# Residual adds moved to GpSimd, an order on its queue, wide PSUM buffers and a new prologue in a fused convolution and phase-mixing kernel

## Chip, cores, metric

One core of a Trainium2 chip. The metric is device time in microseconds (us), the median of several executions. Ratios are the mean time of one kernel's runs over that of the other's runs of the same rounds, so they are not quite the ratio of the medians quoted beside them. The kernel before ran beside each of the three groups of experiments, each group on another chip, and its median there lies between 1477.4 and 1481.4 us. Each kernel was profiled once, so a stretch of a profile stands for one execution.

## The reference, cut to what matters

```python
# x: (8, 4224, 192); weight: (8 heads, 7 taps)
w = softmax(weight)                                  # per head
x = causal 7-tap convolution of x with w, per head   # "attn_out"
theta = x @ w_theta
zr, zi = x * cos(theta), x * sin(theta)
y = w_tok_r @ zr + w_tok_i @ zi                      # over the 4224 tokens
u = x + y
out = u + relu(u @ w_ch)
```

Nearly all arithmetic is the token mix `y`: two 4224 x 4224 matrices against 1536 columns (8 batches x 192).

## The kernel before: the parts that matter

Tokens are cut into 33 chunks of 128. Each chunk is convolved (`conv`), transposed, multiplied by `w_theta`, sent through sine and cosine, and multiplied with x into seven operands `z`. The token mix runs in 58 steps. A step takes up to 11 chunks and two blocks of 128 output rows, by a seven-product scheme whose weight blocks are transposed and combined on VectorE. Partial sums go to `part` in memory and come back 17 steps later. Steps 41 to 57 are final: they add x (the residual add), then cast, transpose and multiply by `w_ch`. TensorE's results land in buffers of the PSUM memory, and VectorE or ScalarE has to copy each out, or "evacuate" it, before this program uses the buffer again. A buffer of one bank holds 512 float32 per partition here.

```python
mmpool = tile_pool(name="mmps", bufs=4, space=PSUM)       # four one-bank buffers
def transposed(u):                                        # 6 transposes, one copy on ScalarE
    tp = bank("tp", F16) ...
# class Step
def load_w(self, name):                                   # four of these a step
    for a in range(NQ):
        nc.gpsimd.dma_start(out=st[...], in_=w[...])      # float32 -> float16, no order given
def add_x(self, i):
    to = part[...][tb] if self.late else self.pv[i]       # late: the last five steps
    nc.gpsimd.dma_start(out=to[:, cols], in_=xs[rows, cols], accum_op=ALU.add)
def give(self, y, i, h, copies):                          # empties an accumulator: pv += y (VectorE)
def cast(self, i, g):
    self.ub[i, g] = wk.tile([P, GC], F16, name="ub", tag="ub", bufs=4)   # ScalarE
def output(self, i, g, k):                                # half of a group: 4 matmuls, 1 VectorE op
# prologue: bands of the convolution by 15 VectorE operations; while the first chunks
# are made, everything that TensorE can't yet do is replaced by idle matmuls on `spare`
```

`in_order("pe" | "dve" | "act", ins)` chains the instructions of those engines in program order. Instructions without it, all of GpSimd's, are placed by the scheduler of the framework.

Of the kernel before, what the change touches and what calls it, by code (L numbers as in the profile page):

```python
# [10 lines left out]
ALU = mybir.AluOpType  # L11
# [5 lines left out]
def kernel(  # L17
# [69 lines left out]
    def act(ins):  # L87
        return in_order("act", ins)

    constp = ctx.enter_context(tc.tile_pool(name="const", bufs=1))  # L90
# [7 lines left out]
        tc.tile_pool(name="mmps", bufs=4, space=bass.MemoryType.PSUM)  # L98
# [7 lines left out]
    def bank(name, dtype=F32):  # L106
        return mmpool.tile([P, PC if dtype == F32 else 2 * PC], dtype,
                           name=name, tag="mm")
# [6 lines left out]
    ident = constp.tile([P, P], F16, name="ident")  # L115

    def channel_weights(w, name):
        R = D - P
        t = constp.tile([P, 4, D], F16, name=name)
        nc.vector.memset(t[:, 1:3, :], 0.0)  # L120
        nc.gpsimd.dma_start(out=t[:, 0, :], in_=w[0:P, :])
        nc.gpsimd.dma_start(out=t[0:R, 1, :], in_=w[P:D, :])
        nc.gpsimd.dma_start(out=t[R:P, 2, :], in_=w[0:R, :])
        nc.gpsimd.dma_start(out=t[:, 3, :], in_=w[R:D, :])
        return t
# [5 lines left out]
    def channel_mix(tT, k, w):  # L131
        v = bank("v")
        for b in range(2):
            for i in range(2):
                pe(nc.tensor.matmul(  # L135
                    v[:, b * D : (b + 1) * D], lhsT=tT[:, 3 * k + b + i, :],
                    rhs=w[:, 2 * b + i, :], start=(i == 0), stop=(i == 1),
                ))
        return v[:, 0 : 2 * D]

    def transposed(u):
        tp = bank("tp", F16)
        for k in range(6):
            pe(nc.tensor.transpose(  # L144
                tp[:, k * P : (k + 1) * P], u[:, k * P : (k + 1) * P], ident
            ))
        uT = wk.tile([P, 6, P], F16, name="uT", tag="uT")
        act(nc.scalar.activation(  # L148
            out=uT[:, :, :].rearrange("p k s -> p (k s)"), in_=tp[:, 0 : 6 * P],
            func=AT.Copy,  # L150
        ))
        return uT
# [3 lines left out]
    class Chunk:  # L156
# [25 lines left out]
        def conv(self, hp):  # L182
            if hp == 0:
                self.z = zpool.tile([P, 7, HN], F16, name="z", tag="z")
                self.x = self.z[:, T2 : T2 + 2, :].rearrange("p t n -> p (t n)")
            pc = bank("pc")
            for hh in range(2):
                h = 2 * hp + hh
                for half in range(2):
                    pe(nc.tensor.matmul(  # L190
                        pc[half * 2 * Q : (half + 1) * 2 * Q,
                           hh * B * G : (hh + 1) * B * G],
                        lhsT=bands[:, h, :, :].rearrange("p a m -> p (a m)"),
                        rhs=self.xw[:, half, :, h * G : (h + 1) * G],
                        start=True, stop=True,
                    ))
            act(nc.scalar.activation(  # L197
                out=self.x.rearrange("p (b d) -> p b d", d=D)[
                    :, :, hp * 2 * G : (hp + 1) * 2 * G
                ].rearrange("p b (h g) -> p h b g", h=2),  # L200
                in_=pc[:, 0 : 2 * B * G].rearrange("p (h b g) -> p h b g", h=2, b=B),
                func=AT.Copy,
            ))
            if hp == H // 2 - 1:
# [6 lines left out]
        def transpose(self, g):  # L211
            self.xT[g] = transposed(self.x[:, g * GC : (g + 1) * GC])

        def theta(self, g, k):
            v = channel_mix(self.xT[g], k, wth).rearrange(
                "p (b h e) -> p b h e", b=2, h=2
            )
            b0 = g * GB + 2 * k
            for first, bias in ((Z11, half_pi[:]), (Z21, None)):
                o = self.z[:, first : first + 2, :].rearrange(  # L220
                    "p h (b e) -> p b h e", e=HD
                )[:, b0 : b0 + 2, :, :]
# [18 lines left out]
        def tasks(self):  # L241

            for hp in (0, 2):
                yield lambda hp=hp: [self.conv(hp), self.conv(hp + 1)]
            for g in range(NG):
                yield lambda g=g: self.transpose(g)
            for g in range(NG):
                for k in range(2):
                    yield lambda g=g, k=k: self.theta(g, k)
# [17 lines left out]
    class Step:  # L267


        def __init__(self, t):  # L270
# [8 lines left out]
            self.blocks = ("11", "21", "22", "12") if self.pair else ("11", "12")  # L279
            self.st, self.w, self.ub, self.uT, self.pv = {}, {}, {}, {}, []  # L280

        def load_w(self, name):
            tb = self.tbs[int(name[0]) - 1]
            w = (moe_w_tok_r, moe_w_tok_i)[int(name[1]) - 1]
            st = wpool.tile([P, NQ, NW * Q], F16, name="st", tag="st", bufs=4)
            n = self.n * Q
            for a in range(NQ):
                t0 = token(self.ks[0], a)
                nc.gpsimd.dma_start(  # L289
                    out=st[a * Q : (a + 1) * Q, :, 0:n],  # L290
                    in_=w[tb * P : (tb + 1) * P, t0 : t0 + n]
                    .rearrange("(bt i) s -> i bt s", bt=NQ),
                )
            self.st[name] = st
# [4 lines left out]
        def turn(self, name):  # L299
# [3 lines left out]
                self.st[name][:, :, 0 : self.n * Q]  # L303
# [35 lines left out]
        def add_x(self, i):  # L339

            if self.late:
                to = part[(self.t // NU - 1) % 2][self.tbs[i], :, :]
            else:
                to = self.pv[i]
            rows = slice(self.tbs[i] * P, (self.tbs[i] + 1) * P)
            for cols in (slice(0, HN), slice(HN, N)) if self.late else (slice(0, N),):
                nc.gpsimd.dma_start(  # L347
                    out=to[:, cols], in_=xs[rows, cols], accum_op=ALU.add
                )
# [61 lines left out]
        def cast(self, i, g):  # L411
            self.ub[i, g] = wk.tile([P, GC], F16, name="ub", tag="ub", bufs=4)
# [7 lines left out]
        def output(self, i, g, k):  # L420
            pk = self.pv[i][:, g * GC + k * 2 * D : g * GC + (k + 1) * 2 * D]
            dve(nc.vector.scalar_tensor_tensor(  # L422
                out=pk, in0=channel_mix(self.uT[i, g], k, wch), scalar=0.0, in1=pk,
                op0=ALU.max, op1=ALU.add,
            ))
            if k == 1:
                rows = slice(self.tbs[i] * P, (self.tbs[i] + 1) * P)
                nc.sync.dma_start(
                    out=out[g * GB : (g + 1) * GB, rows, :].rearrange("b s d -> s b d"),
                    in_=self.pv[i][:, g * GC : (g + 1) * GC].rearrange(  # L430
                        "p (b d) -> p b d", d=D
                    ),
                )

        def outputs(self):
# [3 lines left out]
            for i in range(len(self.tbs)):  # L439
                at = ((-self.time / 7 + 0.6, 1.2) if late else (0.7, 12.7))[i]  # L440
                cast, turn, mix = (1, 2.6, 4.4) if late else (2, 3.6, 5.4)
                for g in range(NG):
# [3 lines left out]
                    for k in range(2):  # L446
                        found.append((d + mix + 0.7 * k,
                                      lambda i=i, g=g, k=k: self.output(i, g, k)))
# [8 lines left out]
    def step_events(t):  # L457
# [11 lines left out]
        if t + 2 < NSTEP:  # L469
            nxt = steps[t + 2]  # L470
            for j, name in enumerate(nxt.blocks):
                found.append(((0.3, 1.3, 2.3, 4.3)[j], lambda name=name: nxt.load_w(name)))
# [4 lines left out]
        if t >= NU - 2:  # L477
# [4 lines left out]
            for k in (k for k in range(NK) if start[k] == t + 1 and k >= NW):  # L482
                pos = [0, .5, 1.3, 1.5, 2.1, 2.3, 2.5, 2.7, 3.1, 3.15, 3.4, 3.6]
# [14 lines left out]
    spare = bank("spare")  # L498
    noise = zpool.tile([P, PC], F16, name="noise", tag="z")
    nc.vector.memset(noise, 0.0)  # L500
    masks = wk.tile([2 * WR, KS, 2, Q], F16, name="masks", tag="ub", bufs=4)
    nc.gpsimd.memset(masks, 1.0)
    for k in range(KS):
        nc.gpsimd.affine_select(
            out=masks[:, k, :, :], in_=masks[:, k, :, :], pattern=[[WR, 2], [1, Q]],
            channel_multiplier=-1, base=HALO - KS + 1 + k,
            compare_op=ALU.is_equal, fill=0.0,
# [3 lines left out]
    for a, lo in ((0, True), (1, False)):  # L511
# [4 lines left out]
        )  # L516
    wmax = constp.tile([P, H], F32, name="wmax")
    nc.vector.tensor_reduce(out=wmax, in_=wsb, axis=mybir.AxisListType.X, op=ALU.max)
    nc.vector.tensor_tensor(
        out=wsb, in0=wsb, in1=wmax[:, :].unsqueeze(2).to_broadcast([P, H, KS]),  # L520
        op=ALU.subtract,
    )
    nc.scalar.activation(out=wsb, in_=wsb, func=AT.Exp)
    nc.scalar.activation(out=wmax[:, 0:1], in_=wsb[:, 0, 0:1], func=AT.Sin)
    wsum = constp.tile([P, H], F32, name="wsum")
    nc.vector.tensor_reduce(out=wsum, in_=wsb, axis=mybir.AxisListType.X, op=ALU.add)
    nc.vector.tensor_scalar_add(out=wsum, in0=wsum, scalar1=1e-9)
    wrcp = constp.tile([P, H], F32, name="wrcp")
    nc.vector.reciprocal(out=wrcp, in_=wsum)
    wbf = constp.tile([P, H, KS], F16, name="wbf")  # L530
    nc.vector.tensor_tensor(
        out=wbf, in0=wsb, in1=wrcp[:, :].unsqueeze(2).to_broadcast([P, H, KS]),
        op=ALU.mult,
    )
    taps = wk.tile([2 * WR, KS, Q], F16, name="taps", tag="uT")
    nc.vector.tensor_tensor(
        out=taps, in0=masks[:, :, 0, :], in1=masks[:, :, 1, :], op=ALU.add
    )
    btmp = wk.tile([2 * WR, 2, H, Q], F16, name="btmp", tag="ub", bufs=4)
    for k in range(KS):  # L540
        nc.vector.tensor_tensor(
            out=btmp[:, 1 if k else 0],
            in0=taps[:, k, :].unsqueeze(1).to_broadcast([2 * WR, H, Q]),
# [124 lines left out]
```

## Time and profile before

| | before |
|---|---|
| time, median | 1480.2 us |
| TensorE busy | 97% of the span |
| idle TensorE | 44 us, plus 16 us of spare matmuls |
| from the last token-mix matmul to the end | 14.0 us |

Read it from TensorE, which is full from 120 us on but for one dip and the tail. Only the idle time of TensorE can be won. The prediction shows the lines.

### The profile page before, as it was taken

What the parts mean: (1) busy time and instruction counts of PE and PEld (TensorE: products, weight loads), DVE (VectorE), ACT (ScalarE), POOL (GpSimd) and SP (SyncE); (2) the same over time, 40 slices, a digit from 0 to 9 for tenths busy, and PEclk for the clock granted to TensorE, in tenths of its full rate; (3) what the DMA queues carried; (4) which work ended last, traced back from release to release, by engine and by line L of the source; (5) the groups of instructions that cost most, each with busy time, mean ns of one, the idle gap of its engine ahead of it and who ended that gap; (6) DMA issues with size and microseconds to landing.
All of it is one profiled execution on the core that took longest, in us unless ns stands there. A gap on an engine that the chain in (4) does not pass through costs nothing.

```text
span 1479.8 us, 25342 instructions
## 1 busy us (share of the span) xinstructions
PE 1435.6 (97%) x10083; PEld 902.6 (61%) x10083; DVE 980.7 (66%) x1120; ACT 385.9 (26%) x664; POOL 604.5 (41%) x1096
## 2 busy tenths in 40 slices
PE   6899999999999999999999999998799999999997
PEld 3565666666666666666666666665466666666665
DVE  5885645454558787775666668778476667666676
ACT  5881111111135353000000015254021212222134
POOL 9743424242444542433324254553444333333330
PEclk9999999999999999999999999999999999999999
DMA  9997757464699999887868699999999989998675
GB/s 130 216 206 148 135 99 153 93 148 94 147 226 220 237 216 256 186 195 173 200 163 208 152 199 213 216 286 293 189 233 253 226 206 224 202 218 189 142 170 158
DMA packets 241318, 281.96 MB, mean 191 GB/s; under 512 B 76336, under 2 KB 209456, under 8 KB 241200
## 3 DMA queue, kind: packets, MB, share of 16 engines
q0 software_dynamic: 173280, 111.20, 54.0%
q1 hardware_dynamic: 67920, 169.14, 32.2%
q8 instruction: 79, 1.29, 0.3%
q14 instruction: 39, 0.32, 0.1%
HBM read 245.49 MB, written 108.13 MB: 239 GB/s over the span
## 4 chain that ended last, share of the span: by engine, by line
PE 84%; DMA 9%; POOL 4%; DVE 2%; issue 1%; ACT 0%; SPq 0%; DVEq 0%; POOLq 0%; ACTq 0%
PE y L394 77%; PE v L135 4%; DMA xw<-in_x_dram 3%; DMA st<-in_moe_w_tok_r_dram 3%; PE tp L144 2%; POOL st L289 2%; DMA st<-in_moe_w_tok_i_dram 2%; PE pc L190 1%; DMA part<-xs 1%; POOL xw L177 1%; DVE pv L359 1%; DMA xw<-xw 0%; DMA part<-pv 0%; DVE z L237 0%; DVE z L231 0%
## 5 line engine op out<-in xcount | busy, mean ns | idle before, releaser
L394 PE MATMUL y<-z,wt 128*128 128x384 f16 x7656 | 1312.1, 327 | 24.7 <-DVE pv L359 19.7
L394 PEld LDWEIGHTS <-wt 128*128 128x128 f16 x7656 | 738.1, 98 | 482.7 <-issue 31.5
L359 DVE TENSOR_TENSOR pv<-y,pv 128x768 f32<-128x768 f32 x324 | 308.9, 953 | 429.5 <-PE y L394 414.5
L289 POOL DMA_DIRECT2D st<-in_moe_w_tok_r_dram x448 | 244.2, 566 | 355.0 <-DVE wt L301 302.9
L289 POOL DMA_DIRECT2D st<-in_moe_w_tok_i_dram x448 | 243.7, 562 | 349.6 <-DVE wt L301 296.4
L301 DVE STREAM_TRANSPOSE wt<-st 128x1408 f16<-128x1408 f16 (+7 forms) x224 | 326.6, 1463 | 10.9 <-DMA st<-in_moe_w_tok_r_dram 8.5
L148 ACT ACTIVATE uT<-tp 128x768 f16<-128x768 f16 x132 | 105.5, 817 | 321.8 <-PE tp L144 321.8
L313 DVE TENSOR_TENSOR wt<-wt 128x1408 f16<-128x1408 f16 (+7 forms) x216 | 173.6, 804 | 10.1 <-PE y L394 6.6
L197 ACT ACTIVATE z<-pc 128x384 f16<-128x384 f32 x132 | 58.4, 504 | 384.2 <-PE pc L190 384.0
L357 ACT ACTIVATE pv<-y 128x768 f32<-128x768 f32 x66 | 53.8, 816 | 275.2 <-PE y L394 274.7
L135 PEld LDWEIGHTS <-uT 128*128 128x128 f16 x1056 | 93.4, 98 | 34.9 <-ACT uT L148 3.8
L177 POOL DMA_DIRECT2D xw<-in_x_dram x132 | 76.7, 594 | 50.5 <-DMA st<-in_moe_w_tok_r_dram 18.1
L422 DVE SCALAR_TENSOR_TENSOR pv<-v,pv 128x384 f32<-128x384 f32 x132 | 71.4, 548 | 24.5 <-PE v L135 24.0
L226 ACT ACTIVATE z<-v,half_pi 128x384 f16<-128x384 f32 x132 | 77.7, 589 | 32.3 <-PE v L135 31.2
L237 DVE TENSOR_TENSOR z<-z 128x768 f16<-128x768 f16 x132 | 73.6, 557 | 7.3 <-DMA xs<-z 2.4
L413 ACT ACTIVATE ub<-pv 128x768 f16<-128x768 f32 x66 | 52.2, 835 | 71.8 <-DVE pv L359 71.7
L135 PE MATMUL v<-wch,uT 128*128 128x192 f16 x528 | 63.8, 246 | 2.6 <-ACT uT L148 2.6
L231 DVE TENSOR_TENSOR z<-z 128x1536 f16<-128x1536 f16 x66 | 60.0, 950 | 9.1 <-ACT z L226 9.0
L226 ACT ACTIVATE z<-v 128x384 f16<-128x384 f32 x132 | 65.5, 497 | 0.0
L135 PE MATMUL v<-wth,uT 128*128 128x192 f16 x528 | 62.5, 248 | 0.8 <-ACT z L226 0.8
L347 POOL DMA_DIRECT2D pv<-xs x24 | 22.1, 935 | 71.6 <-ACT ub L413 29.3
L190 PE MATMUL pc<-xw,bands 96*64 96x192 f16 x528 | 35.4, 254 | 4.4 <-DMA xs<-z 1.9
(45 smaller groups left out, 195.3 us busy)
## 6 DMA issues: line engine op xcount, KB each, us to landing
part<-pv SPq DMA_DIRECT2D x79, 768.0 KB, 4.1
pv<-part SPq DMA_DIRECT2D x79, 768.0 KB, 6.5
out_dram<-pv SPq DMA_DIRECT2D x66, 384.0 KB, 4.5
st<-in_moe_w_tok_r_dram POOLq DMA_DIRECT2D x280, 88.0 KB, 5.1
st<-in_moe_w_tok_i_dram POOLq DMA_DIRECT2D x280, 88.0 KB, 3.9
pv<-xs POOLq DMA_DIRECT2D x24, 768.0 KB, 6.8
xs<-z SPq DMA_DIRECT2D x132, 96.0 KB, 4.6
xw<-in_x_dram POOLq DMA_DIRECT2D x121, 96.0 KB, 4.8
```

Of the source, the lines that this page charges most:

```text
L135: pe(nc.tensor.matmul(v[:, b * D : (b + 1) * D], lhsT=tT[:, 3 * k + b + i, :], rhs=w[:, 2 * b + i, :], start=(i == 0), stop=(i == 1),))
L148: act(nc.scalar.activation(out=uT[:, :, :].rearrange("p k s -> p (k s)"), in_=tp[:, 0 : 6 * P], func=AT.Copy,))
L177: nc.gpsimd.dma_start(out=self.xw[lo : lo + n, h, :, :], in_=x[:, t0 : t0 + n, :].rearrange("b s d -> s b d"),)
L226: act(nc.scalar.activation(**args))
L231: dve(nc.vector.tensor_tensor(out=o, in0=xv, in1=o, op=ALU.mult))
L237: dve(nc.vector.tensor_tensor(out=z[:, o, :], in0=z[:, a, :], in1=z[:, b, :], op=ALU.subtract))
L289: nc.gpsimd.dma_start(out=st[a * Q : (a + 1) * Q, :, 0:n], in_=w[tb * P : (tb + 1) * P, t0 : t0 + n] .rearrange("(bt i) s -> i bt s", bt=NQ),)
L301: dve(nc.vector.transpose(self.w[name][:, 0 : self.n, :, :], self.st[name][:, :, 0 : self.n * Q] .rearrange("p bt (c j) -> p c bt j", j=Q),))
L313: dve(nc.vector.tensor_tensor(out=self.w[name][:, 0 : self.n, :, :], in0=self.w[a][:, 0 : self.n, :, :], in1=self.w[b][:, 0 : self.n, :, : ...
L359: dve(nc.vector.tensor_tensor(out=o, in0=yv, in1=o, op=ALU.add))
L394: pe(nc.tensor.matmul(y[cn][:, q, 0:BH], lhsT=self.w[wn][:, c, :, :].rearrange("p bt i -> p (bt i)"), rhs=chunks[k].z[:, zn, q * BH : (q + ...
L422: dve(nc.vector.scalar_tensor_tensor(out=pk, in0=channel_mix(self.uT[i, g], k, wch), scalar=0.0, in1=pk, op0=ALU.max, op1=ALU.add,))
```

## The change

The intent: keep residual adds out of the DMA engines, let the loads of x pass weight loads, shorten the prologue, and halve the number of evacuations by wider PSUM buffers. The same token-mix matmuls run in the same order. Cut to its core:

```diff
+    def pool(ins):
+        return in_order("pool", ins)
-        tc.tile_pool(name="mmps", bufs=4, space=bass.MemoryType.PSUM)
+        tc.tile_pool(name="mmps", bufs=2, space=bass.MemoryType.PSUM)
-        return mmpool.tile([P, PC if dtype == F32 else 2 * PC], dtype,
+        return mmpool.tile([P, 2, PC if dtype == F32 else 2 * PC], dtype,
   # conv, theta, output: 8 matmuls into one two-bank tile, evacuated by one instruction
+    def evacuate(out, in_, by_dve=False): ...
+            self.xT[g] = transposed(..., 0 < self.k < 3 or (self.k, g) == (0, 1))   # VectorE
-        def load_w(self, name):      # 4 a step, 4 DMAs each, 4 buffers
+        def load_w(self, m):         # 2 a step, 4 DMAs each, 2 buffers twice as large
+                pool(nc.gpsimd.dma_start(...))
+            if not self.late:
+                xr = wk.tile([P, N], F16, name="xr", tag="xr", bufs=1)
+                nc.sync.dma_start(out=xr, in_=xs[rows, :])
+                pool(nc.gpsimd.tensor_tensor(out=self.pv[i], in0=self.pv[i], in1=xr, op=ALU.add))
+                return
+            ... pool(nc.gpsimd.dma_start(out=part[...], in_=xs[...], accum_op=ALU.add))
-            self.ub[i, g] = wk.tile([P, GC], F16, name="ub", tag="ub", bufs=4)
+            self.ub[i, g] = wk.tile([P, GC], F16, name="ub", tag="ub", bufs=2)
   # prologue: bands by 32 small matmuls instead of 15 VectorE operations; w_theta by plain
   # DMA and a VectorE cast
-            if i < 3:
-                idle(left)
+            if i < 2:
+                idle(min(left, 1))
```

## The prediction

> **What bounds the kernel now.** I read the page's busy shares and slices first.
>
> ```profile
> span 1479.8 us, 25342 instructions
> PE 1435.6 (97%) x10083; PEld 902.6 (61%) x10083; DVE 980.7 (66%) x1120; ACT 385.9 (26%) x664; POOL 604.5 (41%) x1096
> PE   6899999999999999999999999998799999999997
> ```
>
> TensorE is the bound. Its idle time is 1479.8 - 1435.6 = 44.2 us, in three places: the first slices, two slices past the middle, the last one. Any gain must come from there, or from matmuls that are no work: the kernel runs 51 matmuls on a tile `spare` to keep TensorE busy while it has no data (16.0 us in the windows). Then windows, cut where chunk 0's first convolution starts (12.2), where chunk 3's starts (35.27), and where TensorE has become full (120); a quiet stretch; and the dip:
>
> ```profile
> core 0: us, PE busy (x) PEld busy (x) DVE busy (x) ACT busy (x) POOL busy (x), PEclk, DMA share, GB/s
> 12.20:35.27 23.07, 20.01 (x162) 11.38 (x162) 9.48 (x17) 16.58 (x35) 21.80 (x41) 0.93 1.06 148
> 35.27:120.00 84.73, 73.67 (x648) 48.51 (x648) 75.05 (x105) 67.92 (x137) 53.24 (x98) 1.00 1.10 212
> 740.00:777.00 37.00, 37.00 (x230) 22.26 (x229) 22.67 (x21) 0.00 (x0) 10.74 (x20) 1.00 0.67 164
> 1023.00:1056.00 33.00, 19.83 (x105) 10.96 (x103) 16.76 (x19) 2.46 (x6) 11.67 (x20) 0.90 1.07 269
> 1056.00:1450.00 394.00, 394.00 (x2868) 259.40 (x2867) 274.91 (x332) 89.27 (x114) 146.70 (x252) 1.00 0.89 204
> ```
>
> The quiet stretch gives 37.00/230 = 160.9 ns for a 128x384 matmul with its weight load hidden, and no idle time: nothing to gain there. The stretch from 1056 to 1450 has none either. So the ledger of lost time is:
> - lead, 0 to 12.2: nothing useful, 12.2 us lost;
> - chunks 0 to 2, 12.2 to 35.27: 20.01 busy, of which the same windows for the spare matmuls show 11.43, so 8.6 useful of 23.07: 14.5 lost;
> - chunks 3 to 10, 35.27 to 120: 84.73 - 73.67 = 11.1 lost;
> - dip, 1023 to 1056: 33.00 - 19.83 = 13.2 lost;
> - tail, 1443 to 1480: 37.00 minus 28.86 busy = 8.1 lost; about 1 us elsewhere.
>
> That is some 60 us, so about 1420 us of useful TensorE work. This floor is not touched by the change: same matmuls, same columns.
>
> The waits of TensorE in the whole run say who ends the idle time, and the timeline of the dip shows the worst one (1045.43):
>
> ```profile
> PE y L394 <- DVE pv L359: 19.7, 11, 6.0
> PE spare L580 <- POOL ident masks.py:199: 6.8, 1, 6.8
> PE y L394 <- DVE z L231: 3.3, 4, 1.5
> ```
> ```profile
> 1044.42 0.96 DVE L359 TENSOR_TENSOR pv<-y,pv 128x768 f32<-128x768 f32 x1 [8.92 <-DMA st<-in_moe_w_tok_i_dram]
> 1045.30 1.63 DVE L301 STREAM_TRANSPOSE wt<-st 128x1408 f16<-128x1408 f16 x1
> 1045.43 5.01 PE L394 MATMUL y<-z,wt 128*128 128x384 f16 x22 [6.04 <-DVE pv L359]
> ```
>
> TensorE waits for VectorE to empty an accumulator, and VectorE sat 8.92 us because weight loads were late. Why late? The source view of the residual adds:
>
> ```profile
> L347 POOL DMA_DIRECT2D pv<-xs x24: 898/912/1260, 1037.4 to 1339.8; - x24
> L347 POOL DMA_DIRECT2D part<-xs x18: 797/1132/2428, 952.8 to 1118.4; - x18
>   POOL st L289: 21.7, 14
> ```
>
> The 18 accumulating DMAs into `part` belong to the last five steps and stand in the program at steps 49 to 53 of 58: a step of this stage takes 29 us (the chain repeats from 1072.8 to 1101.8 to 1130.8) and step 53 starts near 1400, so they stand at some 1290 us or later. They ran from 952.8: nothing ordered GpSimd's queue, so they were hoisted into the stretch that also loads x for the last chunks. Weight-load issues waited 21.7 us behind L347; from 960 to 1050 the DMA view has 286 GB/s and 8 to 9 us to landing for weights, against 122 GB/s and 3.5 to 5.1 between 150 and 400.
>
> **What the Trainium skill says.**
> - "GPSIMD Engine Reference", section "Elementwise — side-by-side cycle accounting": a two-input add costs about 2.6 cycles per element, 4497 ns for 2048 float32. An estimate for 1536 columns: 4497 x 1536/2048 = 3.4 us. The trace of before has no GpSimd add to compare.
> - "SBUF — State Buffer", section "SBUF: two separate sides": GpSimd and VectorE share a port pair under an exclusive lock, which a VectorE op with two SBUF inputs also takes. So an add can hold up a weight sum (L313, 0.8 us) or a product for up to 3.4 us. Before shows no instance.
> - "DMA: Bandwidth & Descriptors", section "Anatomy of one DMA": many descriptors can be emitted before the incremental cost shows. The trace agrees: weight-load issues cost 543 ns at the median, x loads with some two to three times as many rows 582.
> - "TensorE: Matmul & The Clock Gate", section "The HAM clock gate": the clock is halved unless TensorE has been busy for a window of about 3.4 us. The trace agrees in kind: the granted clock is 0.93 from 12.2 to 35.27 and 0.90 in the dip.
>
> **The change, part by part.**
> 1. *Order on GpSimd, and adds there.* Weight loads, late accumulates and the new adds are chained in program order, so the 18 accumulates leave the dip. The 24 direct ones (768 KB) become plain 384 KB loads plus an add. Weight loads merge, 896 issues to about 450, near 0.58 us each: GpSimd saves some 230 us of issue and spends 24 x 3.4 = 82 us on adds. GpSimd doesn't bound steady state (11 of 37 us), so only the dip counts. I keep 3.5 us of its 13.2 for adds that block VectorE and for accumulates now in steps 49 to 53. Gain 9.7.
> 2. *Bands on TensorE.* Before, 15 VectorE operations from 6.61 build the bands, ready at about 12.2. After: the softmax part still ends near 5.5, three small VectorE operations at 0.2 make the taps by 6.4, 32 tiny matmuls at about 0.07 (the 96x64 band loads took 0.31 for eight) take 2.3, the two-engine copy 0.5: 9.5 or so. Gain 2.5.
> 3. *Chunks 0 to 2.* ScalarE is the latency: per chunk 4 copies (0.87 a pair), 8 sines (0.85 a pair, from 28.70 to 29.55), 2 transposed copies (1.51): 6.7 us chained, plus spare matmuls in TensorE's order. After, half of chunk 0's copies and both transposed copies of chunks 1 and 2 go to VectorE, which is free here (9.48 of 23.07), and most spares go. I work the three out as 3.5, 6 and 6.5 us = 16 instead of 23.1, so 7.4 lost instead of 14.5. Chunk 2's load, which TensorE waited 1.5 us for, is issued some 5 us sooner. Gain 7.
> 4. *Chunks 3 to 10.* Two-bank evacuation: a chained 768-column copy is 0.755 against 0.87 for two of 384; per chunk 2 x 0.115 + 4 x 0.1 = 0.6 us less ScalarE. But VectorE is busy 75.05 of 84.73 and loses no work there, and DMA is already at 1.10. Gain 2 of the 11.1.
> 5. *Two wide PSUM buffers instead of four.* Neutral in steady state; in the tail, where transposes and outputs alternate, it costs about 1.
>
> Sum: 9.7 + 2.5 + 7 + 2 - 1 = 20.2; I round up to 23 because the freed GpSimd queue should also bring weights earlier, where VectorE's 90% hides small waits. 1480.2 - 23 = 1457.
>
> **Rivals.**
> - *The adds cost more than the dip gives back.* 24 locks of 3.4 us beside a VectorE that is 70% busy (274.91 of 394). Against it: an accumulator may be emptied up to one run later, 22 x 0.161 = 3.5 us, so most locks are hidden. If each cost 0.5 us, 12 us return: about 1469.
> - *A cold clock.* With few spare matmuls, chunks 0 to 2 may run at half clock: 8.6 useful us become up to 17, partly under ScalarE's latency. Costs up to 6: about 1463.
> - *DMA bounds the start.* For: the chain that ended last runs through x and weight transfers until about 97 us. Against: before 40 us, landing times are only 2.6 to 4.3. Then the gains of 2 to 4 vanish later: about 1468.
> - *All goes well.* Start loss 18 where parts 2 to 4 leave 26, dip and adds nearly nothing: about 1446.
>
> **Range and chances.** Over 2% faster needs less than 1450.6, thus 29.6 us out of a ledger of 60 of which tail and lead keep about 18: it needs the fourth rival. I give it 0.25. A slowdown of 2% would need some 50 us of new waits: 0.02. Range 1445 to 1469.
>
> **What would show it.** Right: no TensorE dip between 950 and 1080; accumulates into `part` only after about 1250; chunk 0's first convolution near 9.7 and chunk 3's near 26; GpSimd adds near 3.4 us; TensorE still full from 120 to the tail. Wrong: TensorE idle behind VectorE in the steps with adds, adds far above 3.4 us, a granted clock well under 0.93 early on, chunk 3's convolution waiting for x, or loss between 35 and 120 grown beyond 11.

## The result, and the profile after

The changed kernel takes 1479.85 us (1479.5 to 1480.68, 4 runs) against 1480.25 us: ratio 0.9999, 95% interval 0.9982 to 1.0016. Nothing was gained. First the page of the kernel after (span, TensorE's busy tenths, its granted clock in tenths):

```profile
span 1478.3 us, 24435 instructions
PE   6899999999999999999999999998999999999996
PEclk7999999999999999999999999999999999999998
```

The dip past the middle is milder, the last slice is emptier, and the first slice has a clock of 0.7. The windows of the kernel after, cut at its own first convolution, at chunk 3's, at 120, and around the dip:

```profile
core 0: us, PE busy (x) PEld busy (x) DVE busy (x) ACT busy (x) POOL busy (x), PEclk, DMA share, GB/s
9.22:34.33 25.11, 17.47 (x137) 10.37 (x138) 13.14 (x24) 11.58 (x15) 16.86 (x30) 0.71 1.26 176
34.33:120.00 85.67, 77.55 (x656) 50.31 (x656) 76.58 (x105) 64.21 (x86) 33.83 (x60) 0.97 0.99 205
1000.00:1056.00 56.00, 48.67 (x346) 30.32 (x345) 48.20 (x45) 15.65 (x20) 24.00 (x26) 0.97 0.91 228
1056.00:1440.00 384.00, 384.00 (x2806) 253.39 (x2805) 311.38 (x268) 87.63 (x113) 143.94 (x151) 1.00 0.84 195
```

Both programs run the same 7656 token-mix matmuls in the same order. So the start of the k-th in one trace can be set against the start of the k-th in the other, which is a better ruler than windows. The view of that line alone gives the first and last start, of the kernel before and of the kernel after:

```profile
L394 PE MATMUL y<-z,wt x7656: 322/326/527, 23.7 to 1465.8; 128*128 128x384 f16 x197
```
```profile
L404 PE MATMUL y<-z,wt x7656: 322/326/528, 23.2 to 1458.1; 128*128 128x384 f16 x197
```

At the last of these matmuls the changed kernel is 7.7 us ahead. At the end it is 1.5 us ahead. The whole account, from the two traces (matmuls counted from 0; each row is the time between two marks):

| stretch | before | after | change | predicted |
|---|---|---|---|---|
| lead, to the first convolution | 12.22 | 9.22 | -3.0 | -2.5 |
| chunks 0 to 2, to chunk 3's first convolution | 23.05 | 25.11 | +2.1 | -7 |
| to token-mix matmul 252 | 79.46 | 79.14 | -0.3 | -2 |
| to matmul 5400 | 905.05 | 906.01 | +1.0 | 0 |
| the dip, to matmul 5600 | 50.92 | 43.11 | -7.8 | -9.7 |
| to the last, matmul 7655 | 395.09 | 395.47 | +0.4 | 0 |
| tail, to the end | 14.04 | 20.25 | +6.2 | +1 |
| sum | 1479.8 | 1478.3 | -1.5 | -20.2 |

So the dip and the lead paid nearly as forecast. The first chunks and the tail took it back. The waits of TensorE in the whole run of the kernel after (total, times, longest) show two kinds that before had little or nothing of:

```profile
PE y L404 <- DVE pv L369: 11.8, 7, 5.2
PE tp L153 <- ACT z L233: 6.3, 10, 1.3
PE v L138 <- ACT uT L148: 4.4, 4, 1.6
PE y L404 <- DVE z L238: 3.1, 3, 1.5
PE v L138 <- ACT z L233: 3.1, 3, 1.2
```

`tp` waits for sines and cosines (L233) although a transpose reads none of their results. What it needs is the PSUM buffer that they still read: with two buffers, a group of matmuls takes the one that the group two places ahead had. In the tail (from 1455 us), ScalarE's waits before and after are:

```profile
ACT uT L148 <- PE tp L144: 9.0, 6, 3.1
ACT ub L413 <- DVE pv L359: 1.4, 2, 1.1
```
```profile
ACT ub L423 <- PE tp L153: 7.7, 4, 3.2
ACT uT L148 <- PE tp L153: 1.9, 1, 1.9
```

Before, no cast (`ub`) waited for a transpose. After, casts do: with two cast buffers, a cast must wait until the transposes of the cast before the last have read theirs. In the dip, VectorE and GpSimd of the kernel after in order of time (lines of other operations left out):

```profile
1028.26 4.98 DVE L238 TENSOR_TENSOR z<-z 128x1536 f16<-128x1536 f16 x2
1029.31 3.10 POOL L351 TENSOR_TENSOR pv<-pv,xr 128x1536 f32<-128x1536 f32 x1
...
1035.54 0.95 DVE L369 TENSOR_TENSOR pv<-y,pv 128x768 f32<-128x768 f32 x1
...
1036.54 1.95 PE L404 MATMUL y<-z,wt 128*128 128x384 f16 x6 [5.20 <-DVE pv L369]
```

Two products that take 1.82 us in e4, where no GpSimd add runs, took 4.98 beside a GpSimd add of 3.10. VectorE was not idle before it emptied the accumulator; it came to it late, and TensorE waited 5.20 us, of which the slowed products made some 3.2.

### The profile page after: what moved, and what is told of

Same layout as the page of the kernel before. It is cut to its first block, busy times and chain, and to the rows that moved or that the text cites. A ratio compares the mean times of both kernels' runs of the same rounds, so it can differ in the third digit from the quotient of the medians.

```text
span 1478.3 us, 24435 instructions
## 1 busy us (share of the span) xinstructions
PE 1435.8 (97%) x10086; PEld 904.9 (61%) x10086; DVE 1030.6 (70%) x1050; ACT 361.8 (24%) x461; POOL 435.3 (29%) x655
## 3 DMA queue, kind: packets, MB, share of 16 engines
HBM read 245.49 MB, written 108.13 MB: 239 GB/s over the span
## 4 chain that ended last, share of the span: by engine, by line
PE 91%; DVE 3%; ACT 2%; DMA 1%; POOL 1%; issue 1%; SPq 0%; DVEq 0%; ACTq 0%; POOLq 0%
PE y L404 82%; PE v L138 5%; PE tp L153 3%; PE pc L196 2%; DVE z L238 1%; ACT z L233 1%; DVE z L244 1%; POOL st L294 1%; DVE pv L369 1%; POOL xw L183 1%; DMA xw<-in_x_dram 1%; DMA part<-pv 0%; DVE wt L319 0%; DMA xw<-xw 0%; DVE wt L307 0%
## 5 line engine op out<-in xcount | busy, mean ns | idle before, releaser
L307 DVE STREAM_TRANSPOSE wt<-st 128x1408 f16<-128x1408 f16 (+7 forms) x224 | 326.4, 1462 | 3.9 <-DMA st<-in_moe_w_tok_r_dram 2.1
L294 POOL DMA_DIRECT2D st<-in_moe_w_tok_r_dram x232 | 132.4, 579 | 490.8 <-DVE wt L307 473.4
L294 POOL DMA_DIRECT2D st<-in_moe_w_tok_i_dram x232 | 132.4, 579 | 473.9 <-DVE wt L307 460.4
L319 DVE TENSOR_TENSOR wt<-wt 128x1408 f16<-128x1408 f16 (+7 forms) x216 | 227.2, 1052 | 10.1 <-PE y L404 6.6
L148 ACT ACTIVATE z<-pc 128x768 f16<-128x768 f32 x65 | 52.8, 812 | 386.5 <-PE pc L196 386.5
L367 ACT ACTIVATE pv<-y 128x768 f32<-128x768 f32 x66 | 53.6, 812 | 278.1 <-PE y L404 271.7
L433 DVE SCALAR_TENSOR_TENSOR pv<-v,pv 128x768 f32<-128x768 f32 x66 | 62.3, 948 | 26.9 <-PE v L138 24.1
L351 POOL TENSOR_TENSOR pv<-pv,xr 128x1536 f32<-128x1536 f32 x24 | 75.5, 3147 | 0.5 <-DMA xr<-xs 0.3
L233 ACT ACTIVATE z<-v,half_pi 128x768 f16<-128x768 f32 x66 | 59.5, 901 | 40.7 <-PE v L138 40.7
L233 ACT ACTIVATE z<-v 128x768 f16<-128x768 f32 x66 | 53.1, 804 | 0.0
L153 PE MATMUL tp<-ident,z 128*128 128x128 f16 x396 | 33.8, 223 | 6.7 <-ACT z L233 6.3
```

The source lines that it names most:

```text
L148: act(nc.scalar.activation(out=out, in_=in_, func=AT.Copy))
L153: pe(nc.tensor.transpose(tp[:, 0, k * P : (k + 1) * P], u[:, k * P : (k + 1) * P], ident))
L233: act(nc.scalar.activation(**args))
L294: pool(nc.gpsimd.dma_start(out=st[a * Q : (a + 1) * Q, 0:nb, :, 0:n] .rearrange("i r bt s -> i (r bt) s"), in_=w[self.tbs[0] * P : (self.t ...
L307: dve(nc.vector.transpose(self.w[name][:, 0 : self.n, :, :], self.st[int(name[1])][:, int(name[0]) - 1, :, 0 : self.n * Q] .rearrange("p b ...
L319: dve(nc.vector.tensor_tensor(out=self.w[name][:, 0 : self.n, :, :], in0=self.w[a][:, 0 : self.n, :, :], in1=self.w[b][:, 0 : self.n, :, : ...
```

## The experiments

Theories: **A**, two wide PSUM buffers instead of four narrow ones make TensorE wait, at the start and in the tail. **B**, the clock falls to half for want of spare matmuls. **C**, GpSimd's adds hold a port that VectorE needs. **D**, the halved cast buffers make the tail. In all tables, "252" is the start of token-mix matmul 252 (before 114.73, after 113.47), "dip" the time from matmul 5400 to 5600 (before 50.92, after 43.11), "tail" the time from the last one to the end (before 14.04, after 20.25).

### e2_onebank, e3_warm, e4_dmaadd, e5_dmaadd_ub4

```diff
# e2_onebank: the changed kernel, conv/theta/output in halves again
-        tc.tile_pool(name="mmps", bufs=2, ...)        # [P, 2, PC]
+        tc.tile_pool(name="mmps", bufs=4, ...)        # [P, PC]
# e3_warm: the changed kernel
-            if i < 2: idle(min(left, 1))
+            if i < 3: idle(left)                      # and idle(12), idle(4) in the prologue
# e4_dmaadd: the changed kernel
-                pool(nc.gpsimd.tensor_tensor(out=self.pv[i], in0=self.pv[i], in1=xr, ...))
+                pool(nc.gpsimd.dma_start(out=self.pv[i], in_=xs[rows, :], accum_op=ALU.add))
# e5_dmaadd_ub4: e4_dmaadd, and
-  name="ub", tag="ub", bufs=2
+  name="ub", tag="ub", bufs=4
```

> The changed kernel with four one-bank PSUM buffers again (convolutions, thetas and outputs in halves, as before); all else as changed. Theory A (two wide buffers are what eats the gain, at the start and in the tail): the tail (last token-mix matmul to the end) falls from 20.2 us to below 17, and chunks 0 to 2 (9.2 to 34.3 us in the changed kernel) take under 22 us instead of 25.1; time about 1471. Theory B (cold clock for want of spare matmuls): the tail hardly moves, chunks 0 to 2 stay within 1 us of 25, time 1478 to 1481.

> The changed kernel with the spare matmuls of before back (all that is left over, chunks 0 to 2, and four after the bands). Theory B (cold clock): half-clock time at the start falls from 20 us to under 7, chunks 0 to 2 take under 22 us, time about 1475. Theory A (PSUM buffers): chunks 0 to 2 stay at 24 to 26 us though the clock is full; time within 1.5 us of the changed kernel. The tail is the same in both.

> The changed kernel with the 24 residual adds as accumulating DMAs again, but still in order with the weight loads. Theory C (GpSimd's adds hold the port that two-input VectorE operations need, and this is the rest of the dip): VectorE's weight sums return from 1.05 to 0.80 us, the 5.2 us wait in the dip goes, time about 1473. Rival (the order on the queue makes the rest of the dip): dip still 5 us or more, time 1478 to 1480.

> As e4_dmaadd, with four cast buffers in the output part instead of two (the room comes from the buffer of the adds). Theory D (the tail grew because a cast waits for the transposes of the cast before the last): tail falls from 20.2 us to about 15, time 5 us below e4_dmaadd. Theory A (PSUM buffers make the tail): tail falls by less than 2 us against e4_dmaadd.

| | time | ratio to before (95%) | 252 | dip | tail |
|---|---|---|---|---|---|
| e2_onebank | 1472.1 | 0.9956 (0.9936 to 0.9977) | 107.26 | 44.50 | 17.25 |
| e3_warm | 1481.05 | 1.0012 (0.9993 to 1.003) | 115.07 | 43.95 | 20.13 |
| e4_dmaadd | 1482.05 | 1.0019 (1.0002 to 1.0036) | 113.71 | 45.16 | 19.80 |
| e5_dmaadd_ub4 | 1477.39 | 0.999 (0.9971 to 1.0008) | 113.64 | 44.26 | 15.76 |

**e2** decides the start: with four buffers the first convolution comes at the same time (9.26), but chunk 3's comes at 28.91 instead of 34.33. The window of e2 between the two:

```profile
9.26:28.91 19.65, 15.26 (x137) 9.32 (x138) 12.48 (x25) 12.08 (x28) 16.69 (x30) 0.84 1.38 182
```

19.65 us against 25.11, with the same number of matmuls recorded (137). In this stretch the changed kernel's transposes waited 2.3 us for sines; in e2 that wait is gone. The granted clock rose from 0.71 to 0.84 without any spare matmul added. Theory A holds for the start: 6.2 us at matmul 252, and 3.0 us of the tail's 6.2. The tail came to 17.25, just short of the "below 17" that I had asked for, so something else is in it.

**e3** speaks against B. The same window of e3, from its first convolution to chunk 3's:

```profile
9.27:34.08 24.81, 19.74 (x161) 11.82 (x161) 13.20 (x25) 11.57 (x15) 16.70 (x30) 0.84 1.28 177
```

The spare matmuls raised the granted clock to 0.84, just what e2 had. Yet the stretch takes 24.81 us and not 19.65, and matmul 252 comes 1.6 us later than in the changed kernel. My expectation of a clock at half for under 7 us was not met (0.84 is not full), so what a full clock would be worth stays unmeasured. The 24 spare matmuls that e3 has more in this stretch also occupy TensorE, so e3 is no clean test of the clock alone. But at the same mean clock e2, with four buffers, is 5.2 us shorter.

**e5** against **e4** shows D: two more cast buffers take the tail from 19.80 to 15.76. Their room comes from the buffer `xr` for the adds, which e4 does not have: by the shapes, `xr` and two cast buffers take 3072 bytes per partition each. So the adds on GpSimd may have cost the cast buffers, too. That the changed kernel has no room for both was not tried.

**e4** half confirms C. The mean of VectorE's weight sums (groups view) is, in the kernels before, after and e4:

```profile
L313 DVE TENSOR_TENSOR wt<-wt 128x1408 f16<-128x1408 f16 (+7 forms) x216 | 173.6, 804 | 10.1 <-PE y L394 6.6
```
```profile
L319 DVE TENSOR_TENSOR wt<-wt 128x1408 f16<-128x1408 f16 (+7 forms) x216 | 227.2, 1052 | 10.1 <-PE y L404 6.6
```
```profile
L319 DVE TENSOR_TENSOR wt<-wt 128x1408 f16<-128x1408 f16 (+7 forms) x216 | 173.6, 804 | 10.1 <-PE y L402 6.6
```

The hold-up is real: 227.2 - 173.6 = 53.6 us of VectorE's time, out of 75.5 us of GpSimd adds, and it goes with the adds. But the time did not improve, and the dip grew by 2 us. In e4's timeline VectorE sat idle before the emptying of an accumulator for another reason:

```profile
1045.33 0.96 DVE L367 TENSOR_TENSOR pv<-y,pv 128x768 f32<-128x768 f32 x1 [10.16 <-issue]
```

The releaser is not named. But the view of the residual add issued at 1027.23 (`--source L349 --window 1027:1028`) gives its landing, 18.0 us later and thus at 1045.2, just before this emptying started:

```profile
L349 POOL DMA_DIRECT2D pv<-xs x1: 986/986/986, 1027.2 to 1027.2; - x1
DMA to landing us min/median/max: 18.0/18.0/18.0
```

I take this landing for what ended the wait; e11 tests it below. So one wait took the place of the other, and my expectation of 1473 failed. The kernel before shows the same at the emptying of 1044.42 that the prediction reads. The weight load that its profile names, issued at 1039.33, landed 5.7 us later, at 1045.05, which is after the emptying had begun. The residual add issued at 1037.45 landed in time:

```profile
L347 POOL DMA_DIRECT2D pv<-xs x1: 912/912/912, 1037.4 to 1037.4; - x1
DMA to landing us min/median/max: 6.9/6.9/6.9
```

The next one, issued at 1040.92, landed 11.5 us later, at 1052.4, and the next emptying that VectorE was idle for started at 1052.46.

### e6_onebank_dmaadd_ub4, e8_onebank_split3_ub3, e9_before_order, e10_onebank_act

```diff
# e6: e2_onebank + e4_dmaadd + four cast buffers
# e8: e2_onebank, and
-                pool(nc.gpsimd.tensor_tensor(... 1536 columns))
+                for c in range(3): pool(nc.gpsimd.tensor_tensor(... 512 columns))
+            if self.late and casts[0] % 3 == 0: use the buffer xr for this cast
# e9: the kernel BEFORE, and nothing but
-                nc.gpsimd.dma_start(...)          # load_w, add_x
+                pool(nc.gpsimd.dma_start(...))
# e10: e2_onebank, and
-  0 < self.k < 3 or (self.k, g) == (0, 1)         # evacuation by VectorE
+  False
```

> One-bank PSUM buffers, accumulating DMAs in order, four cast buffers. If the two causes of the tail add up (casts 4.0 us from e5 against e4, PSUM 3.0 us from e2 against the changed kernel), its tail is 13 to 14 us; the start is that of e2 (matmul 252 near 107.5), the dip that of e4 (8 to 9 us); time 1468 to 1470. If they are one cause measured twice, tail 15 to 16 us.

> e2_onebank with each GpSimd add cut into three of 512 columns, and a third cast buffer in the last steps (the buffer of the adds is free there). Theory C (VectorE is locked out for a whole add): the weight sums' mean falls from 0.95 us to below 0.88, the 5.2 us wait in the dip shrinks to 2 or 3, tail 15 to 16; time about 1467. Rival (VectorE is delayed by the sum of the adds, however cut): weight sums stay at 0.95, dip as before, only the tail gains: 1470.

> The kernel before with nothing but the order: weight loads and accumulating DMAs chained on GpSimd's queue, x loads free. Theory (the hoisted accumulates made the dip of before): accumulates into part start only after 1250 us, weights land in time, dip 5 to 9 us instead of 13.2, time 1473 to 1476. Rival (the dip is that stage's own: the first final step's adds come late whatever the order): dip 11 to 14 us, time 1478 to 1481.

> e2_onebank with the evacuations of the first chunks all on ScalarE again. If the two-engine evacuation carries part of the start's gain: token-mix matmul 252 moves from 107.3 to 109 or later, time about 1474. If it is hidden by other waits: 252 within 0.7 us of 107.3, time 1472.

| | time | ratio to before (95%) | 252 | dip | tail |
|---|---|---|---|---|---|
| e6_onebank_dmaadd_ub4 | 1468.5 | 0.9938 (0.9922 to 0.9955) | 105.86 | 45.37 | 14.13 |
| e8_onebank_split3_ub3 | 1472.3 | 0.9959 (0.9944 to 0.9974) | 105.76 | 44.84 | 15.40 |
| e9_before_order | 1472.04 | 0.9959 (0.9944 to 0.9974) | 113.08 | 43.11 | 14.67 |
| e10_onebank_act | 1471.36 | 0.9955 (0.994 to 0.997) | 108.13 | 44.85 | 17.24 |

**e9** is the plainest result: nothing but the order on GpSimd's queue, put into the kernel before, shortens the dip as much as the whole change does (43.11 in both), and the kernel is faster than the changed one. My expectation held (a dip shorter by 7.8 us), and the time is a little better than the 1473 to 1476 that I had asked for. The accumulates are where they were written, in its trace:

```profile
L350 POOL DMA_DIRECT2D part<-xs x18: 817/1198/1537, 1276.2 to 1389.7; - x18
```

Before, they ran from 952.8 to 1118.4. The first two residual adds are now issued at 1021.63 and 1025.80 instead of 1037.45 and 1040.92, and land at 1034.5 and 1041.3 instead of 1044.3 and 1052.4. GpSimd adds and merged weight loads, the rest of what the change does on that queue, are not needed for this gain.

**e6**: tail 14.13, that of before. Casts and PSUM buffers are two causes, and together they make the whole loss. What remains in its dip is the wait for the accumulating DMA, as in e4 (issued at 1019.38, landed 17.4 us later; the emptying started at 1036.82).

**e8**: the rival held for the weight sums and the dip. Cut in three, the adds take 82.7 us instead of 74.8 in e2, and the weight sums' mean is 961 ns where e2 had 949. The longest wait in the dip fell from 5.2 to 3.8 us, but the dip as a whole is 0.3 us longer than e2's. The third cast buffer gave 1.85 us of tail, but 1.8 us were lost between matmuls 5600 and 7655, where e2 lost nothing. The waits view shows no wait of TensorE there; their cause is open.

**e10**: with the first evacuations back on ScalarE, matmul 252 comes 0.9 us later, between my two expectations. But e10's first convolution happened to come 1.07 us later than e2's (10.33), and the clock differs, too: from 60 to 66 us the granted clock is 0.72 in e10 and in e14 (below), and 1.00 in e6, e8, e11 and e12. e14 keeps VectorE's help and reaches matmul 252 at 108.23, e10 at 108.13; the four others reach it at 105.8 to 106.2. So no gain from VectorE's help shows, and differences of 2 us at this mark go with the clock. The 1.07 us go with TensorE's pace. The 32 band matmuls in the changed kernel and in e10:

```profile
6.51 1.57 PE L566 MATMUL bp<-taps,sel 7*96 7x8 f16 x32 [1.35 <-DVE taps L562]
```
```profile
6.55 2.64 PE L569 MATMUL bp<-taps,sel 7*96 7x8 f16 x32 [1.40 <-DVE taps L565]
```

I take this for the full and the half clock; e10's record of the clock starts only at 16.86 us, and the views count what lies before a record as full. Eight spare matmuls run ahead of them, from 2.41 to 5.15 us in the changed kernel. The same eight (twelve in e3) come before a first convolution at 9.2 to 9.3 us in the changed kernel, e2 and e3, and at 10.3 in the eight other kernels with this prologue. This fits "TensorE: Matmul & The Clock Gate" (section "The HAM clock gate"), which calls the activity window free-running.

### e11_best, e12_coarse, e13_order_fewspare, e14_early_gpsimd

```diff
# e11: e6, and x is added to part of steps 41 and 42 in memory, at steps 29 and 30
+            self.early = self.final and t + NU < NSTEP + 2
-            if not self.late:
+            if not (self.late or self.early):
+        if t + 12 < NSTEP and steps[t + 12].early:
+            for i in range(len(steps[t + 12].tbs)):
+                found.append((3.3 + 1.7 * i, lambda i=i: steps[t + 12].add_x(i)))
# e12: e2_onebank, all 8 matmuls first, both evacuations after
# e13: e9_before_order, and
-            if i < 3: idle(left)
+            if i < 2: idle(min(left, 1))
# e14: e2_onebank + e11's early adds + e8's third cast buffer; GpSimd adds, uncut
```

> e6_onebank_dmaadd_ub4, and x is added to the partial sums of the first two final steps (41 and 42) in memory twelve steps earlier, in a quiet stretch, as for the last five steps. Theory (what is left of the dip, 8.9 us in e6, is the first final step waiting for its residual add): the dip falls to 2 or 3 us, the rest as e6, time 1462 to 1463. Rival (VectorE's products for the last chunks make the dip whatever the add does): dip stays at 6 us or more, time 1467 to 1469.

> e2_onebank with four one-bank buffers, but all matmuls of a pair first and both evacuations after, as the wide buffers have it. If it is the number of buffers that counts: matmul 252 within 1.5 us of e2's 107.3 and tail near 17, time 1472. If it is the coarser grain: matmul 252 near the changed kernel's 113.5, tail near 20, time 1479.

> e9_before_order with the few spare matmuls of the changed kernel. If the spare matmuls of before stand in the way of work: matmul 252 moves from 113.1 to 111 or earlier, time 1470. If they fill time that is lost anyway or keep the clock up: matmul 252 at 112.5 to 114.5, time 1472 to 1473.

> e2_onebank with the early adds of e11 for steps 41 and 42, GpSimd adds for the others and a third cast buffer in the last steps. If the lock of the port costs nothing where VectorE has slack: the dip falls from 7 to 2 or 3 us, nothing is lost from 1060 to 1440, tail 15.4: time 1466. If locks cost time in the later steps too: another 2 us or more are lost there, time 1468 or above.

| | time | ratio to before (95%) | 252 | dip | tail |
|---|---|---|---|---|---|
| e11_best | 1459.44 | 0.9853 (0.9832 to 0.9873) | 105.95 | 36.11 | 14.14 |
| e12_coarse | 1471.48 | 0.9933 (0.9912 to 0.9953) | 106.15 | 43.16 | 18.37 |
| e13_order_fewspare | 1473.54 | 0.9944 (0.9919 to 0.9968) | 113.54 | 43.47 | 14.69 |
| e14_early_gpsimd | 1460.13 | 0.986 (0.9839 to 0.988) | 108.23 | 36.10 | 14.73 |

**e11** beats both kernels. Adding x for the first two final steps long ahead takes the dip from 45.37 (e6) to 36.11. So what was left of the dip in e6 was the first final step waiting for its residual add. The time beat my 1462 to 1463; it is 1.5% below that of the kernel before, still under 2%. The page of e11:

```profile
span 1457.1 us, 24640 instructions
PE   7899999999999999999999999999999999999997
```

**e12** separates the number of buffers from their size. Four buffers with the coarse grain of the change reach matmul 252 at 106.15, where e2 had 107.26 and e6, e8 and e11, with the fine grain, 105.8 to 106.0. At the start it is the number of buffers alone. In the tail, 18.37 lies between e2's 17.25 and the change's 20.25, so there the grain has a part, too.

**e13**: fewer spare matmuls in the prologue change nothing that lasts (113.54 against 113.08). They had filled time that was lost anyway.

**e14**: with the dip out of the way, GpSimd adds and accumulating DMAs do about as well. The dip is 36.10 in both. Between matmuls 5600 and 7655, e14 loses 0.7 us against e11; its weight sums still average 931 ns. It is 2.3 us later at matmul 252 than e11, in a part that its edits don't touch, and this goes with the half clock near 61 us that e11 doesn't have. I had expected 1466 for it; like e11, it did better.

## Why the prediction was wrong

- **What bounds the kernel; the ledger.** Right. The core TensorE work did not change, and all but 1.4 us of what was found or lost lies in the places it named.
- **Part 1, order and adds.** Right that order on the queue takes most of the dip's loss away, a little large: 9.7 forecast, 7.8 measured, and the accumulates now run from 1274.7. e9 shows that the order alone does it. But one step was misread: "VectorE sat 8.92 us because weight loads were late". What VectorE waited for was the residual add of the first final step (landing at 1044.3; the weight load named landed after), which without the order was issued 15.8 us later than with it (e9). So moving the adds to GpSimd is not what helped (e9), and preparing the first ones early is what all but empties the dip (e11, e14). The lock of the port, which the prediction named as a rival, makes some 3.2 of the 5.2 us wait left in the changed kernel's dip; where the adds don't run on GpSimd, a landing takes its place (e4). The rival's main form, a cost in each of the 24 adds, fell: from matmul 5600 to the last one the change lost 0.4 us.
- **Part 2, bands.** Right: 2.5 forecast, 3.0 measured, 1.9 in the eight kernels whose first convolution comes at 10.3.
- **Part 3, chunks 0 to 2.** This step failed: "I work the three out as 3.5, 6 and 6.5 us = 16 instead of 23.1". They took 25.1. I added up ScalarE's durations and never asked for the PSUM buffer each group of matmuls must wait for. With two buffers, a transpose waits for the sines of the group two places ahead. Undoing this alone (e2) gives 19.65, still 3.7 more than forecast; of that rest the cause stays open. VectorE's help, on which the sum counted, doesn't show: without it (e10) the stretch takes 19.35. The halved clock, my rival, is there (0.71), but more buffers raise it without a spare matmul (0.84 in e2), and spare matmuls that raised it as far (e3) left the stretch at 24.81.
- **Part 4, chunks 3 to 10.** Forecast 2, measured 0.3. With four buffers, the same stretch takes 107.26 - 28.91 = 78.35 us instead of 79.14. Fewer ScalarE instructions bought nearly nothing here, where VectorE is busy 76.58 of 85.67 us.
- **Part 5, the tail.** This step failed, too: "it costs about 1", measured 6.2. The prediction counted the PSUM buffers and overlooked the cast buffers in the same diff (`bufs=4` to `bufs=2`). The two shares come to the same end by either road: 20.25 (change), 17.25 (narrow PSUM buffers, e2), 14.13 (and four cast buffers, e6), or 19.80 (e4), 15.76 (four cast buffers, e5), 14.13 (and narrow PSUM buffers, e6). So PSUM made 1.6 to 3.0 us of it and the casts 3.1 to 4.0, depending on which is undone first.
- **Rounding up by 3 us** for weights that come earlier had no ground in the ledger, and nothing came of it.
- **Rivals.** None described what happened: a buffer that is fewer, not slower, and that bites only where TensorE has nothing else to do.
- **Open.** The 1.0 us lost between matmuls 252 and 5400: e2 shows 0.8 of it with four PSUM buffers, and e9, without the other parts, none. So most of it is not in the PSUM buffers; the merged loads and the shifted places of chunk work are left, untested.

## What to carry to other kernels

When a change halves the number of buffers to make each twice as large, follow for each group of matmuls whose release it waits for, above all in the prologue and the tail, where no other work hides the wait. A producer that is not ordered can be hoisted into the busiest stretch; an order on its queue is a small edit here and gave 0.4% by itself. When a profile names a DMA as the end of a wait, check that it had landed, and that the instruction reads what it brings. And when the first use of something comes right where other work peaks, prepare it in a quiet stretch: that was the largest single gain of all (9 us of the dip, e6 against e11).

## What the Trainium skill lacked or had wrong

- "SBUF — State Buffer": the exclusive lock agrees with the traces. Two products took 4.98 us instead of 1.82 beside one GpSimd add of 3.10, and VectorE lost 53.6 us in weight sums over 24 adds (31.3 in e2, with the same adds). What it lacks: cutting the GpSimd operation in three did not help (weight sums 961 ns against 949, adds 82.7 us against 74.8).
- "GPSIMD Engine Reference": its rate gave an estimate of 3.4 us for 1536 columns; with a float16 second operand the add took 3.15 us on average (3.12 in e2).
- "TensorE: Matmul & The Clock Gate": that the window is free-running agrees with the traces: after eight spare matmuls of 384 columns, 32 small matmuls took 1.57 us in some executions and 2.64 in others. More spare matmuls (e3) raised the mean clock of the first chunks from 0.71 to 0.84 and did not shorten them.
- "Trainium Kernel Development and Optimization" (section "Best Practices") recommends double buffering, to overlap DMA with compute. No page weighs more small PSUM buffers against fewer large ones: four buffers of one bank against two of two banks were worth 6.2 us at the start and 3.0 us in the tail.
- No page tells that an unordered DMA of GpSimd's queue can move far ahead of its place: 18 accumulates ran from 952.8 us instead of 1276.2, and ordering them was worth 5 to 8 us.
